# A delta rule with a dense layer behind it: the order of weight loads, of the second block's Y, of a merge step and of the lane copies

## The chip, the cores and the metric

One core of one Trainium2 chip runs the whole kernel. The metric is the device time of one execution in microseconds (us), the median of several runs. The engines are named as in the profile: PE is TensorE (matmuls), PEld its weight loads, ACT is ScalarE, DVE is VectorE, POOL is GpSimd, and SP is the engine that only issues transfers here. ACT and POOL have transfer queues of their own.

## What is computed

Every one of 4x8 heads runs a linear-attention recurrence with the delta rule over 768 steps, with a state of 48x48. Its output, put side by side over the heads, goes through a dense layer of 384 to 2048, a piecewise activation, and a second one back to 384.

```python
k_n = k / (np.linalg.norm(k, axis=-1, keepdims=True) + 1e-06)
for t in range(S):                       # S = 768, state starts at zero
    kt, vt, bt = (k_n[:, :, t], v[:, :, t], beta[:, :, t, None])
    y[:, :, t] = np.einsum('bhd,bhde->bhe', q[:, :, t], state)
    v_old = np.einsum('bhde,bhd->bhe', state, kt)
    state = state + bt[:, :, :, None] * np.einsum('bhd,bhe->bhde', kt, vt - v_old)
x = y.transpose(0, 2, 1, 3).reshape(3072, 384)
h = x @ w_in                             # 384 -> 2048
g = np.where(h >= 1, h, np.where(h <= -1, 0.0, (h + 1) ** 2 / 4))
out = g @ w_out                          # 2048 -> 384
```

All is float32; the dense products are done in three passes over a high and a low part.

## The kernel before

**Blocks and pairs.** Time is cut into 12 blocks of 64 steps, and two blocks make a pair: six pairs, G = 0 to 5. In a block the recurrence becomes a triangular solve and a few products. For every block: the Gram products of the keys (`gram_k`, into GG) and of queries with keys (`gram_q`, into Q); the inverse of a unit triangular 64x64 matrix; and the chain of four products through the state: R (`chain_r`, values less what the state holds), U (`chain_u`), Y (`chain_y`, the output, written as a high and a low part into xb), and D (`chain_d`, the state update). Y needs U; D needs U; the next block's R needs D; U needs R.

**The inverse.** `lanes` copies the 32x32 diagonal parts of GG beside themselves (L266), transposes them to lanes on DVE (L268), computes the norms (with a square root on ACT, L236), scales (L281) and lets POOL cut the triangle (L282). `solve` or `solve_whole` eliminates column by column on DVE (L300 to L313), `unlanes` brings the result back into XT and GG. Then `merge32` joins two 32x32 inverses to one of 64 on PE: its first argument names the block whose first product y1 (L374) is made, its second the block whose second product x2 (L376) is made. y1 is evicted to GG on ACT (L386), and x2 of the same block reads that. x2 is evicted to XT (L381), which U reads. `merge16_a` and `merge16_b` do the same a level below, in the first two pairs only.

**The dense layers.** For each pair there are 16 *items*, one per 128 of the 2048 hidden columns. An item is the up projection (L610, nine matmuls of 512 columns into h), the activation (two passes and a square on ACT, L735 and L754, and a maximum on DVE, L762), the split into ghi (ACT, L730) and glo (DVE, L731), and, two items later, the down projection (L625, twelve matmuls). h has two banks, so an up waits for the maximum of two items before. The first pair has 24 items: eight for its first block alone, eight for both, eight for its second block alone; those for one block are half as wide.

**The order around the items.** All engines take their work in program order. `at(pe, G, t, ...)` puts a product, and `at(fill, G, t, ...)` a piece of other work (a step of a generator, a load), at item t of pair G; t goes in halves. On PE, a product at a whole t stands between the up and the down of that item, one at t + 0.5 stands behind the down. The product at a whole t is evicted in the same item, ahead of the second activation pass; the one at t + 0.5 at the beginning of the next item (`finish(late)`). The fills of the same half stand ahead of the eviction on ACT and DVE. `M` is the item at which the merge steps of the pair begin, 16 in the first pair and 8.5 in the others. While pair G's items run, the recurrence of pair G + 1 is worked off. The solve for the pair after that starts at item -1.5, that is, in the last items of the pair before.

**The seam.** Y of a block goes to xb partly by copies and partly through a small tile, stg, which six transfers on SP's queue (L461) put in their rows: r = 0 and 64, and for each the three parts k. The first up of the next pair reads xb part by part; its first part needs the first and the fourth transfer.

**The prologue.** Before the items, the first two blocks are loaded: K by halves on SP and ACT, Q and KV on SP. The first three of sixteen weight tiles (768 KB each) go on ACT's queue ahead of Q in the program, the next five on SP behind Q. While DVE solves, PE runs 36 holding matmuls (`hold`, L554, 72 instructions) behind the Q-K products. `stage` runs products on PE, then some steps of weight unpacking (`wu`, on ACT and DVE) or of scaling (`sv`), then the evictions. The PSUM tiles `ch` have two banks, which all pieces of the chain take in turn.

Of the kernel before, what the change touches and what calls it, by code (L numbers as in the profile page):

```python
# [24 lines left out]
SOON = 8  # L25
# [6 lines left out]
def delta_rule_moe(ctx: ExitStack, tc: tile.TileContext, kqa, kqb, kv, beta, w, out):  # L32
# [14 lines left out]
    nc = tc.nc  # L47
# [58 lines left out]
    def weight_loads(n0, n1, q=nc.sync):  # L106
        for f in range(n0, n1):
            RAW[f] = const.tile([P, 2, 2 * DM], F32, name=f"wt{f}")
            q.dma_start(out=RAW[f].bitcast(I32), in_=w.bitcast(I32)[:, f])
# [1 line left out]

    load_k(0, (nc.sync, nc.scalar))
    load_k(1, (nc.sync, nc.scalar))
    weight_loads(0, 3, nc.scalar)
    beta_sb = const.tile([P, NS, 32], F32, name="beta_sb")
    nc.sync.dma_start(out=beta_sb[:, 0], in_=beta[:, 0])
    load_q(0)
    load_q(1)
    weight_loads(3, SOON)
    load_kv(0)  # L120
    load_kv(1)
    load_k(2)
# [3 lines left out]
    for c0, base, step, n in ((0, -H, -C, NP), (NP, -C - H - NP, C, NP), (C, -C, C, H)):  # L126
        x = perm[:, 0:C].rearrange("c (a f l) -> c a f l", f=2, l=H)[:, :, :, c0:c0 + NP] if c0 < C else perm[:, C:P].rearrange("c (a f l) -> c a f l", f=2, l=H)
# [29 lines left out]
    GG = const.tile([P, 2, NU, C], F32, name="GG")  # L157
# [30 lines left out]
    def banks(*shape):  # L188
        return [ps.tile([P, H, *shape], F32, **acc()) for _ in range(2)]
# [4 lines left out]
    def gram_k(g):  # L194

        x, b_ = KE.pop(g) if g in KE else K[g], banks(C)
        for j in range(H):
            for e, f in quarters():
                k, o = x[f * C:f * C + D, e * H + j, :], (1 - e) * C
                nc.tensor.matmul(b_[f][o:o + C, j], k, k, start=True, stop=True)  # L200

        def evict():
            for f in range(2):
                nc.scalar.copy(out=GG[:, g % 2, half(f)], in_=b_[f])
        return evict
# [48 lines left out]
    def lanes(G):  # L254

        A = S["A"] = sb.tile([P, 32, 32], F32, name="A", bufs=1)
        if G < WHOLE:
            X = S["X"] = sb.tile([P, 2, 16, 16], F32, name="X", bufs=1)
            Xf = X.rearrange("l s c t -> l (s c t)")
            nc.gpsimd.memset(X, 0.0)  # L260
            for s in range(2):
                nc.gpsimd.memset(Xf[:, 256 * s:256 * s + 256:17], 1.0)
            nc.gpsimd.memset(ZT[:, :, :, 16:32], 0.0)
        for g in range(2):
            for r in (0, C):
                nc.vector.tensor_copy(out=GG[r:r + 32, g, :, 32:64], in_=GG[r:r + 32, g, :, 0:32])  # L266
            yield
        nc.vector.transpose(out=A, in_=GG[:, :, :, 32:64].rearrange("p g u t -> p t (g u)"))  # L268
        yield
        n = sb.tile([P, 32], F32, name="N2")  # L270
        nc.vector.tensor_copy(out=n, in_=A.rearrange("l j t -> l (j t)")[:, 0:1024:33])
        r = norms(n)
        N = S["N"] = sb.tile([P, 32], F32, name="N3")
        nc.vector.transpose(out=N, in_=n)
        gm = S["gm"] = sb.tile([P, 32], F32, name="gm")
        nc.vector.reciprocal(out=r, in_=n)
        nc.vector.tensor_tensor(out=gm, in0=r, in1=beta_sb[:, G, :], op=ALU.mult)
        nc.vector.tensor_tensor(out=gm, in0=gm, in1=r, op=ALU.mult)
        yield
        if G >= WHOLE:  # L280
            nc.vector.scalar_tensor_tensor(out=A, in0=A, scalar=-1.0, in1=gm[:, :, None].broadcast_to([P, 32, 32]), op0=ALU.mult, op1=ALU.mult)  # L281
            nc.gpsimd.affine_select(out=A, in_=A, pattern=[[-1, 32], [1, 32]], base=0, channel_multiplier=0,  # L282
                                    compare_op=ALU.is_gt, fill=0.0)
            nc.gpsimd.memset(A.rearrange("l c t -> l (c t)")[:, 0:1024:33], 1.0)
            return
        A16 = S["A16"] = sb.tile([P, 2, 16, 16], F32, name="A16", bufs=1)
        for s in range(2):
            b = slice(16 * s, 16 * s + 16)
            nc.vector.tensor_tensor(out=A16[:, s], in0=A[:, b, b], in1=gm[:, b, None].broadcast_to([P, 16, 16]), op=ALU.mult)
        X32 = S["X32"] = sb.tile([P, 32, 32], F32, name="A", bufs=1)  # L290
        nc.gpsimd.memset(X32, 0.0)
        yield
# [243 lines left out]
    def stage(pieces, *fill):  # L536
        evicts = products(*pieces)
        for gen, m in fill:
            run(gen, m)
        finish(evicts)  # L540

    spare += START
    wu, sv, ln, raws = unpack(), [scale_v(0), scale_v(1)], lanes(0), []
# [19 lines left out]
    one_ = lambda f, *a: [lambda: f(*a)]  # L563
# [1 line left out]
    stage(one_(merge16_a, 1), (wu, 4))  # L565
    stage(one_(merge16_b, 0), (sv[0], 2), (wu, 2))
    stage(one_(merge16_b, 1), (wu, 4))
    stage(one_(merge32, 0, None, True), (wu, 3))
    stage(one_(merge32, 1, 0, True), (wu, 3))
    stage(one_(merge32, None, 1), (wu, 1), (sv[1], 2))  # L570
    weight_loads(SOON, SOON + 2, nc.scalar)
    stage(both(chain_u, 0), (wu, 2))
    stage(both(chain_y, 0), (wu, 4))
# [61 lines left out]
    pe, fill = {}, {}  # L635

    def at(where, G, t, *x):
        where.setdefault(2 * first[G] + int(round(2 * t)), []).extend(x)

    def lane_steps(G, t, gen, *more):  # L640
        for j in (0,) + (more or (0.5, 1, 1.5, 2)):
            at(fill, G, t + j, (gen, 1))

    def chain(G, t, a):
        for j, f, g in ((0, chain_u, a), (1, chain_y, a), (2, chain_d, a), (3, chain_r, a + 1), (4, chain_u, a + 1), (4.5, chain_y, a + 1), (5.5, chain_d, a + 1)):
            if (f, g) != (chain_d, ntot - 1):
                at(pe, G, t + j, lambda f=f, g=g: f(g))

    def plan(G):

        a, b = 2 * G + 2, 2 * G + 3
        if G == NS - 1:
            return
        va, vb = scale_v(a), scale_v(b)
        if G == 0:
            ln, so, un = lanes(1), solve(), unlanes()
            at(pe, G, 0, lambda: chain_y(1))
            at(fill, G, 0.5, (load_q, 3))
            at(pe, G, 0.5, lambda: chain_d(1))
            at(pe, G, 1, lambda: place_beta(1, NS))  # L660
            at(fill, G, 1, (load_kv, 3))
            at(pe, G, 1.5, lambda: gram_k(a))
            at(pe, G, 2.5, lambda: gram_k(b))
            lane_steps(G, 7, ln)
            for j in range(8):
                at(fill, G, 9.5 + j / 2, (so, 2))
            at(pe, G, 11.5, lambda: gram_q(a))
            at(pe, G, 12.5, lambda: gram_q(b))
            at(fill, G, 13.5, (un, 1))
            at(fill, G, 13.5, (un, 9))  # L670
            for j in range(2):
                at(fill, G, 10 + j, (va, 1))
                at(fill, G, 16 + j, (vb, 1))
            at(pe, G, 13.5, lambda: chain_r(a))
            M = 14
            for j, f in enumerate((merge16_a, merge16_b)):
                for g in range(2):
                    at(pe, G, M + j + g / 2, lambda f=f, g=g: f(g))
            M = 16
            last = 24  # L680
        else:
            so, un = solves.pop(G)
            at(fill, G, 0.5, (va, 1))
            at(fill, G, 1, (va, 1))
            at(pe, G, 2.5, lambda: chain_r(a))
            at(pe, G, 4.5, lambda: gram_q(a))
            at(pe, G, 6, lambda: gram_q(b))
            cost, hs = 0, 0
            for j in range(1, 31):
                at(fill, G, -1.5 + hs / 2, (so, 1))  # L690
                cost += j * (31 - j) + 150
                hs = int(cost / 9461 * 17)
            for j, t in enumerate((7, 7.5, 8, 8)):
                at(fill, G, t, (un, 1))
            at(fill, G, 9, (vb, 1))
            at(fill, G, 9.5, (vb, 1))
            M = 8.5
            last = 16
        for j, x in enumerate(((0, None), (1, 0), (None, 1))):
            at(pe, G, M + j / 2, lambda x=x: merge32(*x))  # L700
        chain(G, M + 1.5, a)
        if G < NS - 2:
            at(fill, G, 6.5 if G else 14, (load_k, a + 2))
            at(fill, G, M + 0.5, (load_k, b + 2, (nc.sync, nc.sync), True))
            at(pe, G, M + 2, lambda: gram_k(a + 2))
            at(pe, G, M + 4, lambda: gram_k(b + 2))
            lane_steps(G, M + 3, lanes(G + 2), 1.5, 2, 2.5, 3)
            solves[G + 1] = solve_whole(), unlanes_whole()
            at(fill, G, M + 3.5, (load_q, a + 2))
            at(fill, G, M + 5, (load_k, b + 2))  # L710
            at(fill, G, M + 7, (load_q, b + 2))
            at(fill, G, last + 0.5, (load_kv, a + 2))
            at(fill, G, last + 1.5, (load_kv, b + 2))

    solves = {}
    for G in range(NS):
        plan(G)
# [20 lines left out]
    for n, item in enumerate(items):  # L738
# [16 lines left out]
        if len(ready) == LAG:  # L755
            x = ready.pop(0)
# [11 lines left out]
    G = NS - 1  # L768
# [50 lines left out]
```

## Time and profile before

| | us |
|---|---|
| runs before, median of 3 | 662.41 |
| runs before, lowest and highest | 660.76, 667.59 |
| profiled execution | 666.11 |
| its span from first to last instruction | 664.4 |
| mean granted TensorE clock | 0.928 |

The profile is of one execution. A busy time is the sum over an engine's instructions, an idle time in brackets is what stood just before the instruction on its engine, with what seems to have released it. A line number is that of the kernel before. The items of the six pairs begin at about 82, 211, 305, 399, 495 and 585 us; in each, PE is busy for nearly all of the time, and the places where it is not are what the prediction quotes.

### The profile page before, as it was taken

The numbers are of one execution on the slowest core, as the hardware profiler recorded it, in microseconds if no ns is written. First come the engines' busy times: TensorE is split into PE (matmuls) and PEld (weight loads), VectorE is DVE, ScalarE is ACT, GpSimd is POOL, SyncE is SP. The second block draws the span as 40 slices with busy tenths as digits, with TensorE's granted clock in tenths as the row PEclk, the third lists the DMA queues.
The fourth block names the chain that finished last, engine by engine and source line by source line (L and its number), as shares of the span: only waits on it lengthen the run. The fifth ranks groups of instructions, "written<-read, shape, count | busy, mean of one in ns | idle before, by whom it ended". The sixth has DMA issues, their size and how long they took to land.

```text
span 664.4 us, 21796 instructions
## 1 busy us (share of the span) xinstructions
PE 605.8 (91%) x9584; PEld 523.5 (79%) x9584; DVE 423.0 (64%) x882; ACT 379.7 (57%) x659; POOL 30.2 (5%) x62
## 2 busy tenths in 40 slices
PE   6985787898897999998999989999979999989996
PEld 5745675687786888887888878888868888879995
DVE  3587969994258894467992577872677854333332
ACT  2315667653754658664569554568545577556663
POOL 2003000000002000010000020000020000000000
PEclk8595679997998999998999998999989999989998
DMA  8720494001022411013400114310214100001001
GB/s 245 280 82 10 165 299 111 8 6 51 9 64 68 113 28 29 17 52 86 110 21 22 42 34 108 93 28 3 66 34 112 38 2 10 6 23 39 0 1 47
DMA packets 32430, 42.54 MB, mean 64 GB/s; under 512 B 7056, under 2 KB 27152, under 8 KB 32336
## 3 DMA queue, kind: packets, MB, share of 16 engines
q1 hardware_dynamic: 30768, 36.64, 19.8%
q10 hardware_dynamic: 1312, 4.42, 2.0%
q8 instruction: 75, 1.23, 0.7%
q14 instruction: 19, 0.16, 0.1%
q0 software_dynamic: 256, 0.08, 0.1%
HBM read 34.05 MB, written 4.72 MB: 58 GB/s over the span
## 4 chain that ended last, share of the span: by engine, by line
PE 67%; DVE 11%; ACT 10%; issue 4%; DMA 4%; SPq 2%; POOL 1%; DVEq 0%; POOLq 0%; ACTq 0%
PE h L610 25%; PE o L625 25%; PE ch L554 4%; PE ch L431 3%; ACT GG L386 2%; ACT XT L381 2%; DMA Q<-in_kqb_dram 2%; ACT XT L388 2%; SPq L461 2%; PE ch L213 2%; PE ch L396 1%; DVE s L762 1%; PE ch L412 1%; ACT s L735 1%; PE ch L200 1%
## 5 line engine op out<-in xcount | busy, mean ns | idle before, releaser
L610 PE MATMUL h<-xb,wt 128*128 128x512 f32 (+1 forms) x936 | 232.8, 395 | 21.1 <-DMA xb<-X 8.4
L610 PEld LDWEIGHTS h<-xb,wt 128*128 128x128 f32 x936 | 170.2, 196 | 55.5 <-issue 9.8
L625 PE MATMUL o<-wt,ghi 128*128 128x384 f32 x768 | 204.1, 348 | 0.0
L625 PEld LDWEIGHTS o<-wt,ghi 128*128 128x128 f32 x768 | 140.7, 193 | 7.4
L762 DVE TENSOR_TENSOR s<-h,s 128x512 f32<-128x512 f32 (+1 forms) x104 | 67.1, 645 | 105.8 <-ACT s L754 105.1
L625 PE MATMUL o<-wt,glo 128*128 128x384 f32 x384 | 131.8, 343 | 0.5 <-DVE glo L731 0.5
L735 ACT ACTIVATE s<-h,half 128x512 f32<-128x512 f32 (+1 forms) x104 | 68.2, 655 | 86.0 <-PE h L610 85.7
L730 ACT CAST ghi<-s 128x512 fp32r<-128x512 f32 (+1 forms) x104 | 61.4, 590 | 83.7 <-DVE s L762 76.4
L731 DVE TENSOR_TENSOR glo<-s,ghi 128x512 fp32r<-128x512 f32 (+1 forms) x104 | 67.0, 644 | 54.5 <-ACT ghi L730 54.4
L625 PEld LDWEIGHTS o<-wt,glo 128*128 128x128 f32 x384 | 74.0, 193 | 2.2 <-DVE glo L731 2.2
L735 ACT ACTIVATE s<-s,one 128x512 f32<-128x512 f32 (+1 forms) x104 | 72.1, 693 | 2.6
L754 ACT ACTIVATE s<-s 128x512 f32<-128x512 f32 (+1 forms) x104 | 62.3, 599 | 3.3
L311 DVE TENSOR_TENSOR pr<-A 128x30 f32<-128x30 f32 (+14 forms) x120 | 39.4, 328 | 6.3 <-POOL A L282 4.5
L313 DVE TENSOR_TENSOR A<-A,pr 128x30 f32<-128x30 f32 (+14 forms) x120 | 39.9, 332 | 4.4
L431 PEld LDWEIGHTS ch<-Q,SU 64*64 64x64 f32 (+3 forms) x1056 | 24.0, 142 | 5.0 <-issue 1.3
L431 PE MATMUL ch<-Q,SU 64*64 64x64 f32 (+3 forms) x1056 | 26.3, 230 | 1.1 <-ACT SU L416 1.1
L457 DVE TENSOR_TENSOR xb<-ch,xb 128x384 fp32r<-128x384 f32 x22 | 12.2, 552 | 19.3 <-ACT X L452 14.4
L554 PE MATMUL ch<-SU 128*128 128x64 f32 (+1 forms) x72 | 24.4, 528 | 0.0
L376 PE MATMUL ch<-GG 32*32 32x32 f32 x768 | 18.2, 200 | 5.0 <-ACT GG L386 5.0
L554 PEld LDWEIGHTS ch<-SU 128*128 128x128 f32 x72 | 15.3, 281 | 8.4 <-issue 8.3
L376 PEld LDWEIGHTS ch<-GG 32*32 32x32 f32 x768 | 15.9, 113 | 7.3 <-ACT GG L386 7.3
L451 ACT CAST xb<-ch 128x384 fp32r<-128x384 f32 x22 | 10.7, 489 | 17.9 <-PE ch L431 17.9
(128 smaller groups left out, 600.7 us busy)
## 6 DMA issues: line engine op xcount, KB each, us to landing
wt<-in_w_dram SPq DMA_DIRECT2D x11, 768.0 KB, 7.0
out_dram<-wx SPq DMA_DIRECT2D x47, 96.0 KB, 2.2
wt<-in_w_dram ACTq DMA_DIRECT2D x5, 768.0 KB, 6.9
KV<-in_kv_dram SPq DMA_DIRECT2D x36, 96.0 KB, 2.4
KV<-in_kv_dram SPq DMA_DIRECT2D x72, 48.0 KB, 2.3
KV<-in_kv_dram SPq DMA_DIRECT2D x12, 192.0 KB, 2.7
xb<-X SPq DMA_DIRECT2D x66, 32.0 KB, 2.0
K<-in_kqb_dram SPq DMA_DIRECT2D x12, 128.0 KB, 3.1
```

Source lines behind the costliest of these rows:

```text
L311: nc.vector.tensor_tensor(out=pr, in0=A[:, 0:n, j:j + 1].broadcast_to([P, n, m]), in1=A[:, j:j + 1, j + 1:32].broadcast_to([P, n, m]), op= ...
L313: nc.vector.tensor_tensor(out=A[:, 0:n, j + 1:32], in0=A[:, 0:n, j + 1:32], in1=pr, op=ALU.add)
L376: nc.tensor.matmul(x2[r:r + 32, u], GG[r:r + 32, gb, u, 32:64], GG[r:r + 32, gb, u, 0:32], start=True, stop=True)
L431: nc.tensor.matmul(yy[i][o * C:o * C + C, e, p], SF[rows, u:u + C], w_[rows, x, k, :], **how)
L554: nc.tensor.matmul(idle[:, 0:m], SF[:, 0:P], SF[:, 0:m], start=True, stop=True)
L610: nc.tensor.matmul(h[:, cols(bs)], WT[f][:, 0, x, k * P:(k + 1) * P], XB[G][:, y, k, cols(bs)], start=(n == 0), stop=(n == 8))
L625: nc.tensor.matmul(oacc[G, k], (ghi, glo)[x][:, k * P:(k + 1) * P], WT[f][:, 1, y, :], start=(new and n == 0), stop=(left[G, b] == 0 and n ...
L730: nc.scalar.copy(out=ghi[:, c], in_=s[:, c])
L731: nc.vector.tensor_tensor(out=glo[:, c], in0=s[:, c], in1=ghi[:, c], op=ALU.subtract)
L735: nc.scalar.activation(out=out, in_=in_, func=AF.Relu, bias=bias, scale=scale)
L754: nc.scalar.activation(out=s[:, c], in_=s[:, c], func=AF.Square)
L762: nc.vector.tensor_tensor(out=s[:, c], in0=h[:, c], in1=s[:, c], op=ALU.max)
```

## The change

Nothing that is computed changes. The edits:

- The weight tiles 0 to 2 leave ACT's queue; tiles 0 to 7 are all loaded on SP, behind Q.
- `lanes` makes its four copies per pair on ACT rather than DVE, except in the prologue.
- In the prologue, three merge stages become four: the first products of both blocks, then the second ones, with the same number of weight steps over all.
- In the items, `merge32(None, 1)` moves from M + 1 to M + 2.5. The chain, still beginning at M + 1.5, has all that follows its first U half an item earlier: the second block's Y comes at item 14 in the later pairs, where it was 14.5.
- The Gram products of the keys for the pair after next come an item and half an item earlier, the first lane step an item, and two loads of Q half an item.
- In pair 1 the solve begins at -0.5 rather than -1.5, its steps spread over 15 half items rather than 17.

```diff
     load_k(1, (nc.sync, nc.scalar))
-    weight_loads(0, 3, nc.scalar)
     beta_sb = const.tile([P, NS, 32], F32, name="beta_sb")
...
     load_q(1)
-    weight_loads(3, SOON)
+    weight_loads(0, SOON)
...
-                nc.vector.tensor_copy(out=GG[r:r + 32, g, :, 32:64], in_=GG[r:r + 32, g, :, 0:32])
+                (nc.scalar.copy if G else nc.vector.tensor_copy)(out=GG[r:r + 32, g, :, 32:64], in_=GG[r:r + 32, g, :, 0:32])
...
-    stage(one_(merge32, 0, None, True), (wu, 3))
-    stage(one_(merge32, 1, 0, True), (wu, 3))
-    stage(one_(merge32, None, 1), (wu, 1), (sv[1], 2))
+    stage(one_(merge32, 0, None, True), (wu, 2))
+    stage(one_(merge32, 1, None, True), (wu, 2))
+    stage(one_(merge32, None, 0), (wu, 3))
+    stage(one_(merge32, None, 1), (sv[1], 2))
...
-        for j, f, g in ((0, chain_u, a), (1, chain_y, a), (2, chain_d, a), (3, chain_r, a + 1), (4, chain_u, a + 1), (4.5, chain_y, a + 1), (5.5, chain_d, a + 1)):
+        for j, f, g in ((0, chain_u, a), (0.5, chain_y, a), (1.5, chain_d, a), (2.5, chain_r, a + 1), (3.5, chain_u, a + 1), (4, chain_y, a + 1), (5, chain_d, a + 1)):
...
-                at(fill, G, -1.5 + hs / 2, (so, 1))
+                at(fill, G, (-0.5 if G == 1 else -1.5) + hs / 2, (so, 1))
                 cost += j * (31 - j) + 150
-                hs = int(cost / 9461 * 17)
+                hs = int(cost / 9461 * (15 if G == 1 else 17))
...
-        for j, x in enumerate(((0, None), (1, 0), (None, 1))):
-            at(pe, G, M + j / 2, lambda x=x: merge32(*x))
+        for j, x in ((0, (0, None)), (0.5, (1, 0)), (2.5, (None, 1))):
+            at(pe, G, M + j, lambda x=x: merge32(*x))
...
-            at(pe, G, M + 2, lambda: gram_k(a + 2))
-            at(pe, G, M + 4, lambda: gram_k(b + 2))
-            lane_steps(G, M + 3, lanes(G + 2), 1.5, 2, 2.5, 3)
+            at(pe, G, M + 1, lambda: gram_k(a + 2))
+            at(pe, G, M + 3.5, lambda: gram_k(b + 2))
+            lane_steps(G, M + 2, lanes(G + 2), 2.5, 3, 3.5, 4)
...
-            at(fill, G, M + 3.5, (load_q, a + 2))
+            at(fill, G, M + 3, (load_q, a + 2))
             at(fill, G, M + 5, (load_k, b + 2))
-            at(fill, G, M + 7, (load_q, b + 2))
+            at(fill, G, M + 6.5, (load_q, b + 2))
```

## The prediction

> **What bounds the kernel now.** I read the page first, then the windows, the timeline at the seams between the pairs of blocks, and the chain of waits.
>
> ```profile
> PE 605.8 (91%) x9584; PEld 523.5 (79%) x9584; DVE 423.0 (64%) x882; ACT 379.7 (57%) x659; POOL 30.2 (5%) x62
> ```
>
> TensorE is busy for 605.8 of 664.4 us, so some 59 us of idle time, and the time at a lower clock, are what a new order can win. The windows (columns: stretch, its length, then busy time of PE, PEld, DVE, ACT, POOL, granted clock, DMA share, GB/s) say where:
>
> ```profile
> 20.00:45.00 25.00, 25.00 (x115) 15.83 (x111) 21.07 (x55) 3.43 (x6) 0.96 (x1) 0.74 0.67 228
> 110.00:120.00 10.00, 6.30 (x35) 4.80 (x35) 9.93 (x16) 6.61 (x14) 0.00 (x0) 1.00 0.34 89
> 170.00:180.00 10.00, 8.82 (x238) 7.81 (x241) 1.79 (x4) 9.18 (x17) 0.00 (x0) 1.00 0.01 3
> 304.00:399.00 95.00, 90.91 (x1424) 78.98 (x1424) 65.60 (x145) 57.07 (x97) 3.51 (x6) 0.98 0.20 54
> ```
>
> A later pair (304 to 399) has 4.1 us of idle PE in 95. Nearly all of it lies at the seam to the next pair. Here is the seam from the second pair to the third, by engine:
>
> ```profile
> 293.57 2.24 PE L431 MATMUL ch<-Q,SU 112*64 112x64 f32 x96
> 295.75 2.34 PE L610 MATMUL h<-xb,wt 128*128 128x512 f32 x9
> 300.10 1.57 PE L473 MATMUL ch<-SU,KV 64*48 64x48 f32 x64
> 304.72 3.20 PE L610 MATMUL h<-xb,wt 128*128 128x512 f32 x9 [3.05 <-DMA xb<-X]
> ...
> 295.85 0.48 ACT L451 CAST xb<-ch 128x384 fp32r<-128x384 f32 x1 [1.71 <-PE ch L431]
> ...
> 294.78 1.22 DVE L281 SCALAR_TENSOR_TENSOR A<-A,gm 128x1024 f32<-128x1024 f32 x1
> 297.51 0.19 DVE L311 TENSOR_TENSOR pr<-A 128x30 f32<-128x30 f32 x1 [1.50 <-POOL A L282]
> 298.98 0.55 DVE L457 TENSOR_TENSOR xb<-ch,xb 128x384 fp32r<-128x384 f32 x1
> ...
> 300.46 3.88 SPq L461 DMA_DIRECT2D xb<-X  x6
> ```
>
> Y's products end at 295.81 and ScalarE starts on them at once, but VectorE's half (L457) waits in its queue behind L281, the wait for GpSimd's select, and three solve steps, until 298.98. So the six transfers start at 300.46, 4.65 us after Y. The next pair's first up projection needs the fourth of them. The other seams and the chain of waits:
>
> ```profile
> 211.11 3.32 PE L610 MATMUL h<-xb,wt 128*128 128x512 f32 x7 [2.54 <-DVE SU L488]
> ...
> 399.15 4.18 PE L610 MATMUL h<-xb,wt 128*128 128x512 f32 x9 [3.00 <-issue]
> ...
> 495.11 4.18 PE L610 MATMUL h<-xb,wt 128*128 128x512 f32 x9 [3.46 <-DMA xb<-X]
> ...
> 585.16 3.66 PE L610 MATMUL h<-xb,wt 128*128 128x512 f32 x9 [1.86 <-DMA xb<-X]
> ```
>
> ```profile
> 302.47 2.01 DMA xb<-X
> ...
> 307.93 2.76 PE o L625 x12
> 310.69 2.10 PE h L610 x9
> 312.79 2.08 PE o L625 x12
> ...
> 403.33 2.85 PE o L625 x12
> ...
> 499.29 2.66 PE o L625 x12
> ...
> 588.82 2.30 PE o L625 x12
> ```
>
> The wait is paid twice: after it the first up takes 3.20 to 4.18 us where 2.10 is usual, and the first down 2.30 to 2.85 where 2.08 is. Those are matmuls at a halved clock (4.18 is twice 2.09). The extra is 1.10+0.68, 2.08+0.77, 2.08+0.58 and 1.56+0.22 us at the last four seams: 1.78, 2.85, 2.66 and 1.78.
>
> **The prologue.**
>
> ```profile
> 6.01 1.62 ACTq L109 DMA_DIRECT2D wt<-in_w_dram  x3
> ...
> 4.26 0.47 SPq L87 DMA_DIRECT2D Q<-in_kqb_dram  x1
> ...
> 14.58 0.66 SPq L92 DMA_DIRECT2D Q<-in_kqa_dram  x1
> 17.70 2.58 SPq L109 DMA_DIRECT2D wt<-in_w_dram  x5
> 20.32 1.45 SPq L98 DMA_DIRECT2D KV<-in_kv_dram  x1
> ...
> 33.37 0.60 SPq L98 DMA_DIRECT2D KV<-in_kv_dram  x1
> ...
> 37.20 0.58 SPq L101 DMA_DIRECT2D KV<-in_kv_dram  x1
> ...
> 20.38 24.45 PE L554 MATMUL ch<-SU 128*128 128x64 f32 x72
> ...
> 22.25 0.18 DVE L237 TENSOR_SCALAR r<-y 128x32 f32<-128x32 f32 x1 [8.12 <-ACT y L236]
> 44.73 1.02 DVE L248 TENSOR_TENSOR KV<-KV,N 128x384 f32<-128x384 f32 x2
> ```
>
> ```profile
> q10 hardware_dynamic: 232, 1.31, 89.6%
> q1 hardware_dynamic: 157, 0.14, 11.6%
> ```
>
> The last fence is the DMA view from 10 to 14 us. Three weight tiles on ACT's queue (q10) hold the engines, SP's queue (q1) with Q gets a ninth, and Q's last issue comes only at 14.58. VectorE idles 8.12 us and the holding matmuls (L554) begin only at 20.38. The weight unpacking that fills VectorE later (9.93 of 10 us between 110 and 120) is placed by program order behind the same work, so what the prologue wins passes through it.
>
> **The change, part by part.** *Weights on SP behind Q.* Q's twelve issues run from 4.26 on. Alone on the engines they should be spaced as the seven of KV from 33.37 to 37.20: 0.64 us. The last is then issued at about 11.3, not 14.58. If the 5.80 us from there to the holds (14.58 to 20.38) stay, the holds start at 17.1, 3.3 us earlier; if Q lands as fast as xb later (2.01) and half of its products, an estimated 1.2, are left, at 14.6, 5.8 earlier. Nothing at all is won if the holds, at a mean clock of 0.74 between 20 and 45, stay at the halved clock so much longer: bounds 0 and 5.8. I take 5.0, nearer the upper end, for those 5.80 us contain the crowding that goes (11.6% of the engines for q1). Eight weights then stand ahead of KV on SP: at the most 3 x 0.52 (2.58 over 5) = 1.5 us of issue. KV is first used at 44.73, without a wait, now near 39.7; its first transfers were issued at 20.32. That cover is large, so nothing.
> [...]
>
> *Four merge stages for three in the prologue.*
>
> ```profile
> 63.61 0.31 PE L376 MATMUL ch<-GG 32*32 32x32 f32 x2 [1.85 <-ACT GG L386]
> ```
>
> The second block's first product no longer carries the first block's second, so ScalarE frees GG sooner and this 1.85 us wait shrinks. But the weight steps (same 30 in all) and an XT copy now stand before U: a gain between -1 and 1.85; I take 1.0.
>
> *Y of the second block at item 14.* It moves ahead of a down projection: 2.08 us earlier on PE. Its evictions come before L281, the select and the solve. Between Y's end and the transfers stand two of ScalarE's four casts (the first 0.48 us), what is left of the norms on VectorE, and VectorE's own four operations (298.98 to 300.46, 1.5 us): an estimated 3.4, where 4.65 were. The fourth transfer is issued 2.0 later and lands after 2.01: Y's end + 7.4, and PE sees it at 7.6. PE's own work in between is now down, up, state update, down: 2.08+2.10+1.57+2.08 = 7.8. The wait is gone with 0.2 to spare, and with it the halved clock. What is late next is VectorE around the seam (state update, three to four solve steps, the max that frees h): I charge 0.5 us a seam, bounds 0 and 1.5. So: second to third 3.05+1.78-0.5 = 4.3; 399: 3.00+2.85-0.5 = 5.35; 495: 3.46+2.66-0.5 = 5.6; 585, where no solve stands by: 1.86+1.78 = 3.6. Sum 18.9.
> The first seam (211) follows half-wide items. There Y moves past half a down, 1.04 us, and the norms stay ahead of it on VectorE: I take 1.5 (bounds 0 and 2.54), with the halved clock left in.
> [...]
>
> *Chain half an item earlier, merge step behind the first Y, Gram steps and loads earlier.* PE does the same instructions. U and Y of the first block now stand apart by one down (2.08 us), as the second block's do, and each other piece by an up or down that covers its eviction. In the half-wide items of the first pair one cover is 1.05, so U to Y and Y to the merge lose a little: I take -1.0, bounds -3 and 1. SP meets each load behind Y's transfers as before: nothing.
>
> *Lane copies.*
>
> ```profile
> L266 DVE COPY GG<-GG 32x512 f32<-32x512 f32 x24 | 9.9, 413 | 7.2 <-ACT GG L204 6.9
> L388 ACT COPY XT<-XT 32x512 f32<-32x512 f32 x20 | 12.3, 616 | 0.4
> ```
>
> Twenty copies leave VectorE (8.3 us) for ScalarE (20 x 0.616 = 12.3). ScalarE has 38 us free in a pair of 95, so nothing on the path beyond the norms' delay counted above.
> *Third pair's solve an item later.* Thirty steps over 15 half items for 17, same end: nothing.
>
> Sum: 5.0+1.0+18.9+1.5-1.0 = 25.4 us. The profiled execution took 666.11 (span 664.4 and 1.7 around it) and would take 640.7. It stands 0.56% above the median of 662.41, from which the sum gives 637.0, my forecast.
>
> **The rivals.** *Y's transfers still come last* (chance 0.18). The margin of 0.2 rests on VectorE's norms, which wait for ScalarE, now with copies in its queue. If the transfers are 2 us later at the three seams with a solve, 1.9 us of wait and the halved clock (2.43 on average) stay: 3 x 4.3 = 13 less, 650. For it: L457 sat 1.9 us behind other work already. Against: L281 and the select go behind it.
> *The prologue gains nothing* (0.10): the holds run longer by what they start earlier. 662.4-19.4 = 643. For it: the clock of 0.74; against: it is the same 72 matmuls.
> *ScalarE becomes the bound, and the kernel is slower* (0.06). Copies and Y's eviction stand ahead of the second activation of the same item, whose square releases the max that frees h. If all is on the path, 12.3 + 5 x 1.2 = 18 us are added, the seams win nothing, the prologue's 6 stay: 674. It decides where ScalarE is above nine tenths busy. For it: 9.18 of 10 us between 170 and 180; against: 57 of 95 in later pairs.
>
> **How the numbers follow.** The forecast, 637 (own range 630 to 645), has 0.60; the rivals 0.18, 0.10 and 0.06; 0.06 is for mixtures about no change. The lower end takes the first seam's clock (2.9, as at 399), the seam charge (1.5) and two to three us of the prologue and first pair: 629. The upper end is the first rival with 2 us: 652. About 1%, 6.6 us, is what a measurement of this kernel can tell from no change: faster 0.87, within it 0.08, slower 0.05.
>
> **What would show it.** Right: hold matmuls from about 15; VectorE's wait for L236 near 2 us; no PE wait above 0.5 us and clock 1.0 at the last four seams; up after the seam at 2.1; Y's transfers issued some 3.4 us after Y. Wrong: a wait for xb that stays, a new one for L762 or on ch at items 9 to 12, holds that end at 45, ScalarE full in the first pair's tail.

## The result and the profile after

| | time, median (lowest to highest) | profiled execution | its span | granted clock |
|---|---|---|---|---|
| before | 662.01 us (660.76 to 667.59) | 666.11 us | 664.4 us | 0.928 |
| changed | 640.32 us (639.83 to 641.19) | 640.05 us | 638.3 us | 0.954 |

The ratio is 0.9658, with a 95% interval of 0.9602 to 0.9714: 21.7 us less on the medians, 26.1 us between the two profiled executions. Of the changed kernel's page, first the busy times, then the TensorE clock in 40 slices (tenths), and below it the clock of the kernel before:

```profile
PE 596.0 (93%) x9584; PEld 514.9 (81%) x9584; DVE 413.8 (65%) x862; ACT 389.9 (61%) x679; POOL 29.7 (5%) x62
...
PEclk8685579999999999999999999999999999999999
...
PEclk8595679997998999998999998999989999989998
```

PE's busy time fell by 9.8 us although it does the same 9584 matmuls: that goes with the lower clock, whose dips past the first slices are gone. Its idle time fell by 16 us. The windows (columns as before) say in which stretches:

```profile
20.00:45.00 25.00, 23.16 (x422) 14.09 (x422) 20.12 (x45) 3.88 (x7) 0.30 (x1) 0.84 0.67 227
110.00:120.00 10.00, 8.14 (x37) 6.09 (x35) 7.53 (x11) 8.12 (x16) 0.00 (x0) 1.00 0.03 8
170.00:180.00 10.00, 9.63 (x257) 8.73 (x256) 4.05 (x10) 8.81 (x22) 0.00 (x0) 1.00 0.18 43
304.00:399.00 95.00, 93.45 (x1502) 80.61 (x1502) 66.97 (x148) 61.54 (x105) 3.51 (x6) 1.00 0.23 60
```

The 95 us of the later pairs hold 93.45 us of PE for 90.91, at a clock of 1.00 for 0.98. The seam from the second pair to the third, by engine:

```profile
282.47 2.24 PE L430 MATMUL ch<-Q,SU 112*64 112x64 f32 x96
...
284.64 0.62 PE L625 MATMUL o<-wt,ghi 128*128 128x384 f32 x2
284.75 0.48 ACT L450 CAST xb<-ch 128x384 fp32r<-128x384 f32 x1 [0.80 <-PE ch L430]
...
286.07 0.55 DVE L456 TENSOR_TENSOR xb<-ch,xb 128x384 fp32r<-128x384 f32 x1
...
286.83 2.24 PE L610 MATMUL h<-xb,wt 128*128 128x512 f32 x9
...
287.55 3.87 SPq L460 DMA_DIRECT2D xb<-X  x6
288.00 1.21 DVE L280 SCALAR_TENSOR_TENSOR A<-A,gm 128x1024 f32<-128x1024 f32 x1
...
289.00 1.15 PE L472 MATMUL ch<-SU,KV 64*48 64x48 f32 x64
...
290.72 0.19 DVE L310 TENSOR_TENSOR pr<-A 128x30 f32<-128x30 f32 x1 [1.51 <-POOL A L281]
...
292.27 2.26 PE L610 MATMUL h<-xb,wt 128*128 128x512 f32 x9
```

(Line numbers up to some L609 are one lower than before.) VectorE's half of Y's eviction, L456, now stands ahead of L280 and the wait for GpSimd, so the six transfers start at 287.55, 2.8 us after Y's end (4.65 before), and the up at 292.27 waits for nothing: the fourth transfer, which it needs, lands at 291.77, half a microsecond ahead. The next three seams and the first one:

```profile
201.86 2.34 PE L610 MATMUL h<-xb,wt 128*128 128x512 f32 x9 [1.26 <-DVE A L312]
...
383.06 2.26 PE L610 MATMUL h<-xb,wt 128*128 128x512 f32 x9
...
474.53 2.33 PE L610 MATMUL h<-xb,wt 128*128 128x512 f32 x9 [0.49 <-DVE glo L731]
...
560.69 2.29 PE L610 MATMUL h<-xb,wt 128*128 128x512 f32 x9
```

No up of 3 to 4 us is left, and three seams are free of a wait for xb. At the other two a short one remains. The profile puts these waits of 1.26 and 0.49 us down to VectorE, but what came last was a transfer, as the same kernel run again shows:

```profile
202.52 2.35 PE L610 MATMUL h<-xb,wt 128*128 128x512 f32 x9 [1.06 <-DVE pr L310]
...
474.82 2.34 PE L610 MATMUL h<-xb,wt 128*128 128x512 f32 x9 [0.53 <-DVE glo L731]
```

There the fourth transfer, issued at 200.35 and 471.41, lands at 202.32 and 474.73, 0.2 and 0.1 us ahead of these ups; in the kernel before, at the first seam, it lands at 210.91, 0.2 ahead of the up at 211.11. At 471.41 it takes 3.3 us to land rather than 2.0. Why is open. The clock stays up at both (1.00 from 200 to 206 and from 473 to 479 us in the changed kernel). The prologue:

```profile
11.32 0.42 SPq L92 DMA_DIRECT2D Q<-in_kqa_dram  x1
11.78 5.01 SPq L109 DMA_DIRECT2D wt<-in_w_dram  x8
14.46 9.75 PE L553 MATMUL ch<-SU 128*128 128x64 f32 x41
16.33 0.18 DVE L236 TENSOR_SCALAR r<-y 128x32 f32<-128x32 f32 x1 [3.43 <-ACT y L235]
38.81 1.02 DVE L247 TENSOR_TENSOR KV<-KV,N 128x384 f32<-128x384 f32 x2
```

Q's last issue is at 11.32 for 14.58, the holding matmuls begin at 14.46 for 20.38, and KV, behind eight weights on SP, is still used without a wait.

What is new on the path stands some two items behind a seam, first at 208 to 214, behind the first seam, then at 303, behind the second:

```profile
208.32 0.56 DVE L247 TENSOR_TENSOR KV<-KV,N 128x384 f32<-128x384 f32 x1 [1.25 <-DMA KV<-in_kv_dram]
...
213.59 0.55 DVE L631 COPY wx<-o 128x384 f32<-128x384 f32 x1
...
214.19 0.62 PE L625 MATMUL o<-wt,ghi 128*128 128x384 f32 x2 [1.77 <-DVE wx L631]
...
303.33 0.62 PE L625 MATMUL o<-wt,ghi 128*128 128x384 f32 x2 [0.42 <-ACT wx L631]
...
303.93 1.01 DVE L631 COPY wx<-o 128x384 f32<-128x384 f32 x2
304.54 0.61 PE L625 MATMUL o<-wt,ghi 128*128 128x384 f32 x2 [0.42 <-DVE wx L631]
```

The down that opens the next pair's accumulators waits for the copies (L631) that store the pair before. VectorE reaches them late, behind solve steps, and at 208 behind KV's landing too. The start of every up, before minus after, gives where the 26.1 us came from:

| stretch (items) | forecast | gain |
|---|---|---|
| to the first up (81.65 to 75.41) | 5.0 + 1.0 | 6.2 |
| first pair (0 to 23) | -1.0 | 0.5 |
| first seam (23 to 26) | 1.5 | 5.2 |
| behind it: KV and store (26 to 28) | 0 | -2.4 |
| second to third pair (28 to 43) | 4.3 | 3.1 |
| third to fourth (43 to 59) | 5.35 | 4.7 |
| fourth to fifth (59 to 75) | 5.6 | 5.0 |
| fifth to last (75 to 91) | 3.6 | 3.7 |
| sum | 25.4 | 26.1 |

### The profile page after: what moved, and what is told of

It is laid out like the page before. It is cut to its first block, busy times and chain, and to the rows that moved or that the text cites. A ratio compares the mean times of both kernels' runs of the same rounds, so it can differ in the third digit from the quotient of the medians.

```text
span 638.3 us, 21794 instructions
## 1 busy us (share of the span) xinstructions
PE 596.0 (93%) x9584; PEld 514.9 (81%) x9584; DVE 413.8 (65%) x862; ACT 389.9 (61%) x679; POOL 29.7 (5%) x62
## 3 DMA queue, kind: packets, MB, share of 16 engines
q10 hardware_dynamic: 880, 2.07, 1.0%
## 4 chain that ended last, share of the span: by engine, by line
PE 57%; DVE 21%; ACT 10%; issue 6%; DMA 3%; SPq 2%; POOL 1%; DVEq 0%; ACTq 0%
PE o L625 20%; PE h L610 18%; PE ch L553 4%; PE ch L430 3%; DVE glo L731 3%; DVE pr L310 3%; DVE A L312 2%; DVE s L762 2%; ACT s L735 2%; ACT GG L385 2%; PE ch L395 2%; ACT XT L387 2%; PE ch L375 2%; DVE SU L487 1%; DVE A L267 1%
## 5 line engine op out<-in xcount | busy, mean ns | idle before, releaser
L610 PE MATMUL h<-xb,wt 128*128 128x512 f32 (+1 forms) x936 | 226.1, 387 | 8.5 <-DVE s L762 5.8
L625 PE MATMUL o<-wt,ghi 128*128 128x384 f32 x768 | 200.9, 343 | 3.9 <-DVE wx L631 3.0
L610 PEld LDWEIGHTS h<-xb,wt 128*128 128x128 f32 x936 | 165.4, 191 | 41.6 <-DVE s L762 7.8
L625 PEld LDWEIGHTS o<-wt,ghi 128*128 128x128 f32 x768 | 137.2, 189 | 12.9 <-DVE wx L631 4.3
L625 PE MATMUL o<-wt,glo 128*128 128x384 f32 x384 | 130.3, 339 | 0.6 <-DVE glo L731 0.5
L625 PEld LDWEIGHTS o<-wt,glo 128*128 128x128 f32 x384 | 72.4, 189 | 2.3 <-DVE glo L731 2.3
L456 DVE TENSOR_TENSOR xb<-ch,xb 128x384 fp32r<-128x384 f32 x22 | 12.1, 551 | 14.5 <-ACT X L451 10.2
L226 DVE TENSOR_TENSOR Q<-ch,mask 64x512 f32<-64x512 f32 (+1 forms) x30 | 20.6, 687 | 0.4
L281 POOL TENSOR_SCALAR_AFFINE_SELECT A<-A 128x1024 f32<-128x1024 f32 x4 | 5.1, 1264 | 299.5 <-DMA xb<-X 261.1
L487 DVE TENSOR_TENSOR SU<-ch,SU 48x384 f32<-48x384 f32 (+1 forms) x30 | 16.6, 555 | 0.7 <-PE ch L472 0.3
```

Source lines behind the costliest of these rows:

```text
L487: nc.vector.tensor_tensor(out=x, in0=y, in1=x, op=ALU.add)
L610: nc.tensor.matmul(h[:, cols(bs)], WT[f][:, 0, x, k * P:(k + 1) * P], XB[G][:, y, k, cols(bs)], start=(n == 0), stop=(n == 8))
L625: nc.tensor.matmul(oacc[G, k], (ghi, glo)[x][:, k * P:(k + 1) * P], WT[f][:, 1, y, :], start=(new and n == 0), stop=(left[G, b] == 0 and n ...
```

## The experiments

Each stands beside runs of the kernel before on its own chip; each "changed kernel" below is the one that this document is about.

**Weights back on ScalarE's queue.** The prologue alone is undone, in the changed kernel:

```diff
+    weight_loads(0, 3, nc.scalar)
     beta_sb = ...
-    weight_loads(0, SOON)
+    weight_loads(3, SOON)
```

> The changed kernel (640.3 us) with weight tiles 0 to 2 back on ACT's queue ahead of Q. Theory: Q lands late again, the holding matmuls begin near 20 us instead of 14.5, and all that follows moves with them: about 646 (645 to 647.5), with the first up near 81.5. Rival: the time up to the first up is set by VectorE's weight unpacking or by PE's own issue, so that an earlier Q is only waited for later: 640 to 642.

648.32 us (645.45 to 649.52), ratio 0.9762 (0.9712 to 0.9811). Its timeline:

```profile
20.49 3.89 PE L554 MATMUL ch<-SU 128*128 128x64 f32 x17
...
22.36 0.18 DVE L237 TENSOR_SCALAR r<-y 128x32 f32<-128x32 f32 x1 [8.17 <-ACT y L236]
```

The 8.17 us wait and the late holds are back, the first up comes at 81.72, 6.3 us later, and the end is 8.0 us later on the median. The time is 0.8 us above the band, and the first up is where it was expected. Where three transfers are issued is, in these profiled executions, the whole of the prologue's gain. In the profiled execution the end is 9.5 us later; the three beyond the 6.3 lie behind the first seam; what takes them is not shown.

**Y half an item later.** The changed kernel, with the second block's U, Y and D back at their old times:

```diff
-... (3.5, chain_u, a + 1), (4, chain_y, a + 1), (5, chain_d, a + 1)
+... (4, chain_u, a + 1), (4.5, chain_y, a + 1), (5.5, chain_d, a + 1)
```

> The changed kernel with U, Y and D of the second block half an item later again (14, 14.5 and 15.5), all else as changed. Theory: at four seams VectorE's half of Y stands behind L281, the select and three solve steps again, PE waits some 3 us for xb and the clock halves: 13 to 17 us more, 653 to 658, the clock lower at each of the last four seams. Rival: the gain at the seams came from the other moves (lane copies on ScalarE, the merge step), Y alone gives only its 2 us at a few seams: 642 to 646.

662.84 us (656.99 to 666.26), ratio 0.9979 (0.9941 to 1.0017): 22.5 us for half an item, and nothing left of the gain although the prologue keeps its six. The direction was expected, not the size. The second seam of this kernel, on PE, VectorE and SP's queue:

```profile
286.79 2.28 PE L430 MATMUL ch<-Q,SU 112*64 112x64 f32 x96 [0.23 <-ACT SU L415]
289.16 1.22 DVE L280 SCALAR_TENSOR_TENSOR A<-A,gm 128x1024 f32<-128x1024 f32 x1
...
291.88 0.19 DVE L310 TENSOR_TENSOR pr<-A 128x30 f32<-128x30 f32 x1 [1.50 <-POOL A L281]
...
293.36 0.55 DVE L456 TENSOR_TENSOR xb<-ch,xb 128x384 fp32r<-128x384 f32 x1
...
294.83 2.60 SPq L460 DMA_DIRECT2D xb<-X  x4
```

```profile
299.09 2.47 PE L610 MATMUL h<-xb,wt 128*128 128x512 f32 x5 [3.04 <-DMA xb<-X]
```

L456 is behind L280, the select and three solve steps again, the transfers start 5.8 us after Y's end, and the wait of 3.04 us is there. Against the changed kernel this one loses 2.0 us up to behind the first seam, then 5.5, 5.0, 6.9 and 3.6 at the four later seams: 21.0, where the prediction had 18.9 for them and the change won 16.5 (table above). So with the other moves in place the old time of Y is 4.5 us worse there than the kernel before, which takes most of the prologue's six as well: L456 ends up 4.3 us behind Y's end, where L457 stood 3.2 behind it before, and at three seams the state update (L472) waits for the eviction too, 0.8 to 1.0 us and again 0.4. That Y half an item earlier (with its U and D) is what removes these waits, lower clock and all (five products of the up at 299.09 take 2.47 us, where the changed kernel's nine at 292.27 take 2.26), is shown.

**Only the chain's times, in the kernel before.**

```diff
-... (1, chain_y, a), (2, chain_d, a), (3, chain_r, a + 1), (4, chain_u, a + 1), (4.5, chain_y, a + 1), ...
+... (0.5, chain_y, a), (1.5, chain_d, a), (2.5, chain_r, a + 1), (3.5, chain_u, a + 1), (4, chain_y, a + 1), ...
```

> The kernel before with the chain's new times alone (first Y, D, R, U, Y, D half an item earlier); weights, merges, lanes, Gram steps, loads and solve as before. Theory: this part carries the seams, 13 to 17 us: 645 to 649, and no PE wait above 1 us at the last four seams. Rival: it needs the moved merge step and the copies on ScalarE, for without them ch or VectorE makes PE wait at items 10 to 13 instead: 653 to 660.

663.01 us (659.99 to 666.12), ratio 0.9984 (0.9956 to 1.0013): nothing. The theory fell. The rival is right that PE waits on ch instead, but its band ended 3 us lower, and its copies on ScalarE turn out not to be needed (next run). Its timeline in the second pair's items, and a row of its waits (total, times, longest):

```profile
268.35 2.24 PE L431 MATMUL ch<-Q,SU 112*64 112x64 f32 x96
...
271.98 0.55 DVE L457 TENSOR_TENSOR xb<-ch,xb 128x384 fp32r<-128x384 f32 x1
272.16 0.30 PE L200 MATMUL ch<-K 48*64 48x64 f32 x2 [1.57 <-issue]
272.82 1.50 PE L200 MATMUL ch<-K 48*64 48x64 f32 x62 [0.37 <-issue]
274.25 2.07 PE L610 MATMUL h<-xb,wt 128*128 128x512 f32 x4
```

```profile
PE ch L200 <- issue: 7.7, 8, 1.6
```

The waits at the four later seams are gone here too. But Y of the first block and the Gram product gram_k (L200) now fall into the same half item, and gram_k has to wait until Y's result has been read out of the same ch banks. The profile names no releaser, but VectorE's two readings of Y end (L458) at 272.06 and 272.72, each 0.1 us ahead of a start of gram_k. Behind the two at 272 the clock falls (0.88 from 268 to 282 us, where the changed kernel has 1.00 from 260 to 274), four products of the up at 274.25 take 2.07 us, and what the seams win is lost in mid-pair.

**All of the new order, in the kernel before.** As the last one, and with the merge step, Gram products, lane steps and loads at their new places; prologue, lane copies and the third pair's solve stay old:

```diff
+        for j, x in ((0, (0, None)), (0.5, (1, 0)), (2.5, (None, 1))):
+            at(pe, G, M + j, lambda x=x: merge32(*x))
...
+            at(pe, G, M + 1, lambda: gram_k(a + 2))
+            at(pe, G, M + 3.5, lambda: gram_k(b + 2))
```

> The kernel before with all of the new order of the pairs (chain half an item earlier, the third merge step behind the first Y, the Gram products, lane steps and loads at their new places), but with its old prologue, its lane copies on VectorE and the old solve of the third pair. Theory: the order is one thing; with the Gram and merge moves beside the chain's times the pairs win what they won in the changed kernel, and only the prologue's 6.2 us are missing: no wait of PE above 0.6 us for Gram's banks (L200), clock 1.0 at the last four seams, first up near 81.7, time 645.5 to 649. Rival, that the lane copies on ScalarE or the later solve are needed for it: ScalarE's or VectorE's lateness brings a wait at the seams or at the lane steps back, 650 to 658.

644.84 us (643.87 to 646.64), ratio 0.9703 (0.9654 to 0.9753), below the band by less than a microsecond. The same 95 us of its windows, and the prologue on PE:

```profile
304.00:399.00 95.00, 93.74 (x1444) 80.71 (x1444) 68.74 (x153) 60.04 (x103) 3.51 (x6) 1.00 0.22 58
```

```profile
13.90 1.68 PE L213 MATMUL o<-Q,K 48*64 48x64 f32 x32 [3.79 <-DMA Q<-in_kqb_dram]
```

The order wins the seams by itself: 93.74 us of PE, clock 1.00; in the old prologue PE still waits 3.79 us for Q. The moves that the prediction priced at nothing or less (Gram, the merge step, lane steps and loads) are worth 18 us together with the chain's times, and those times without them are worth nothing. Which of these moves is needed was not run apart; the waits of the last run point at Gram. The first up comes at 82.03, 6.6 us behind the changed kernel; 4.4 of it are left at the end, most of the difference because here no 1.77 us wait for a store stands at 214.

**Lane copies back on VectorE,** in the changed kernel:

```diff
-                (nc.scalar.copy if G else nc.vector.tensor_copy)(out=GG...
+                nc.vector.tensor_copy(out=GG...
```

> The changed kernel with the lane copies back on VectorE in all pairs. Theory: at the copies' items both engines have gaps, and the norms may even start 1 us earlier; VectorE is not full before the seam: 639.5 to 641.5. Rival: VectorE's 1.65 us more per pair arrive at the seam, where the state update and the solve already delay the maximum and the stores: 642 to 646, with longer PE waits at items 0 to 2 of each pair.

640.19 us (638.70 to 641.91), ratio 0.9646 (0.9600 to 0.9693): no difference, as the prediction had it.

**Three merge stages in the prologue,** in the changed kernel:

```diff
-    stage(one_(merge32, 0, None, True), (wu, 2))
-    stage(one_(merge32, 1, None, True), (wu, 2))
-    stage(one_(merge32, None, 0), (wu, 3))
-    stage(one_(merge32, None, 1), (sv[1], 2))
+    stage(one_(merge32, 0, None, True), (wu, 3))
+    stage(one_(merge32, 1, 0, True), (wu, 3))
+    stage(one_(merge32, None, 1), (wu, 1), (sv[1], 2))
```

> The changed kernel with the three old merge stages of the prologue in place of four. Rival, the prediction's term: the first up comes 1.0 us later (76.4) and the time is 641.3. Theory after the traces: the fourth stage's gain is there at the first U (some 1.2 us) and is lost again in the gaps of 0.9 and 1.4 us without a releaser ahead of Y and U, so the first up starts within 0.4 us of 75.4 and the time is 640 to 640.8.

641.75 us (641.27 to 643.52), ratio 0.9660 (0.9617 to 0.9704). Its timeline, and then the changed kernel's:

```profile
57.17 0.31 PE L375 MATMUL ch<-GG 32*32 32x32 f32 x2 [1.85 <-ACT GG L385]
...
72.22 2.07 PE L411 MATMUL h<-KV,XT 64*64 64x48 f32 x64 [2.44 <-issue]
75.21 2.29 PE L609 MATMUL h<-xb,wt 128*128 128x256 f32 x9 [0.92 <-ACT SU L415]
```

```profile
72.41 2.07 PE L411 MATMUL h<-KV,XT 64*64 64x48 f32 x64 [1.44 <-issue]
75.41 2.29 PE L610 MATMUL h<-xb,wt 128*128 128x256 f32 x9 [0.92 <-ACT SU L415]
```

The 1.85 us wait for GG is back, and yet the first up is not later, as the theory had it. The time, 640 to 640.8 by that theory, is 1.2 to 1.4 us above the changed kernel's two medians, near the 641.3 of the prediction's term, but they were not run beside this one on its chip, and against the kernel before on its own chip the ratio of 0.9660 is within 0.001 of the changed kernel's 0.9658 and 0.9653. The profile can't decide it either, since the first up comes anywhere from 74.4 to 76.5 in the profiled executions that share the changed weight loads, and this execution also lost the clock at 147 (0.84 us for two products of a down at 147.91, where 0.51 is usual). What the fourth stage is worth, nothing or a microsecond, is open.

**The new wait: all store copies on ScalarE,** for the first four pairs of the changed kernel, alone and together with an earlier load:

```diff
-            (nc.scalar.copy, nc.vector.tensor_copy)[k % 2](out=o[:, k % 2], in_=oacc[G, k])
+            (nc.scalar.copy if G < NS - 1 else (nc.scalar.copy, nc.vector.tensor_copy)[k % 2])(out=o[:, k % 2], ...
...
-            at(fill, G, last + 0.5, (load_kv, a + 2))
+            at(fill, G, last + 0.5 if G else 21.5, (load_kv, a + 2))
```

> The changed kernel with all four store copies of the first four pairs (L631) on ScalarE in place of two on ScalarE and two on VectorE. Theory: at the seams a down waits for the store's copy on VectorE, which stands behind the norms and the solve there (0.42 us twice a seam in the trace, some 1.4 us with what surrounds it); ScalarE has room, so the wait for L631 falls below 0.3 us a seam and the time by 2 to 4 us, to 636.5 to 638.5. Rival: ScalarE's casts and evictions then stand behind four copies (4 x 0.47 us), the wait only changes its engine, and the time is 640 to 642.

> The last one with the first pair's load of KV (a+2) issued at item 21.5 rather than 24.5 as well. Theory: VectorE's 1.25 us wait for KV at 208 and the 1.77 us wait of PE at 214 behind it go, so that the gain of 12 us over the kernel before that items 25 and 26 show is kept past item 27 (9.55 there in the changed kernel): 1 to 2.4 us below the run with the store copies alone. Rival: the earlier load meets the transfers of Y at the first seam on the queue or the store's copy is late for another reason; no difference above 0.5 us.

The copies alone: 640.03 us (638.38 to 642.13), ratio 0.9627 (0.9586 to 0.9669). Both: 637.76 us (637.38 to 639.77), ratio 0.9599 (0.9559 to 0.9639). A group of the first one's page (busy, mean, idle before it):

```profile
L625 PE MATMUL o<-wt,ghi 128*128 128x384 f32 x768 | 201.3, 344 | 0.8 <-ACT wx L631 0.8
```

The wait for L631 fell from 3.9 to 0.8 us, and each of three seams won 0.6 to 0.7 us, half of the 1.4 that the theory had. The time did not follow: in the profiled execution the clock fell at 170 and at 249 (the Gram products at 170.07 took 1.97 us, 1.15 in the changed kernel; the up at 248.24 took 3.89), in the first and the second pair, and the two stretches lost 2.6 us each, more than the seams won; whether this edit or chance brings that is open. The band up to 638.5 was missed by the copies alone. With the early load the time is 2.3 us lower on the same chip, as that theory had it, though the two ranges overlap.

**The load alone, and the copies on ScalarE in the later pairs only,** with the changed kernel once more on the same chip:

```diff
-            (nc.scalar.copy, nc.vector.tensor_copy)[k % 2](...
+            (nc.scalar.copy if 0 < G < NS - 1 else (nc.scalar.copy, nc.vector.tensor_copy)[k % 2])(...
```

> The changed kernel once more, beside the next three on the same chip, so that differences of some 2 us can be read against it. Both theories: 639.5 to 641.5. [...]

> The changed kernel with the load of KV (a+2) of the first pair at item 21.5 rather than 24.5, and nothing else. Theory: VectorE's waits for KV at 208 and 212 (1.25 and 0.74 us) go, with them PE's 1.77 us wait for the store's copy at 214, and the time is 1 to 2.4 us below the changed kernel's, 638 to 639.5. Rival: the gain at 638 of the run with both edits comes from the stores alone, and this one equals the changed kernel.

> The early load of KV, and the store copies on ScalarE for the second, third and fourth pair only; the first pair's stay as they were. Theory: the three seams win 0.65 us each as in the runs before, KV's wait wins up to 2.4, and ScalarE's late squares of the half-wide items (VectorE waits 3.6 us for L754 near 205 in the run with all of them) are avoided: 1.5 to 4 us below the changed kernel's, 636 to 638.5. Rival: the same as the run with all pairs' copies on ScalarE, 637.5 to 638.5.

| kernel | time | ratio (95% interval) |
|---|---|---|
| changed, again | 640.54 us (639.00 to 641.75) | 0.9653 (0.9624 to 0.9683) |
| KV earlier | 639.90 us (637.74 to 641.96) | 0.9643 (0.9612 to 0.9673) |
| KV earlier, later pairs' copies on ScalarE | 637.03 us (636.45 to 641.39) | 0.9611 (0.9580 to 0.9642) |

The early load by itself misses its band by 0.4 us and can't be told from the changed kernel in time, though the 1.77 us wait at 214 is gone from its trace: its profiled execution lost as much to a lower clock at 170 (the Gram products at 169.84 took 1.86 us, 1.15 in the changed kernel). With the later pairs' copies five of six runs are below all six of the changed kernel, by 3.5 us on the medians; the two intervals overlap, so that it is faster is likely rather than settled, and it can't be told from the run with all copies on ScalarE and the early load (637.76 us on another chip, ratio 0.9599). Against the changed kernel's first profile the ups gain 2.2 us up to item 27 and 0.6, 0.7 and 0.7 where the store's copies stood behind three seams.

**Third pair's solve begun earlier,** as in the kernel before:

```diff
-                at(fill, G, (-0.5 if G == 1 else -1.5) + hs / 2, (so, 1))
+                at(fill, G, -1.5 + hs / 2, (so, 1))
...
-                hs = int(cost / 9461 * (15 if G == 1 else 17))
+                hs = int(cost / 9461 * 17)
```

> The changed kernel with the third pair's solve begun an item earlier, over 17 half items as in the kernel before. The prediction's term: nothing, within 0.5 us of the changed kernel's. Rival: its steps then stand ahead of Y's evictions and of the store's copies on VectorE in the first seam's items, as they do at the other seams, and 0.5 to 2 us are lost near 200 to 215.

639.09 us (638.34 to 640.84), ratio 0.9634 (0.9605 to 0.9664). The rival's sign is wrong: the store's wait near 215 is 0.32 us here, not longer, perhaps since with the later start more of the long steps stand ahead of that copy. 1.4 us on the medians, with overlapping runs: at the edge of what can be told, and if anything a small loss by the later solve. The prediction's term of nothing, within 0.5 us, is not met by the medians.

## Why the prediction was right, and where it was not

The forecast was 637.0 with a range of 629 to 652; the time is 640.32. The profiled execution was to fall to 640.7 and fell to 640.05. Step by step:

- **Weights on SP** (5.0): right. Holds were put at 14.6 at best and 17.1 at worst and began at 14.46, Q's last issue at 11.3 and came at 11.32. The term was a microsecond short, since the upper bound of 5.8 was what the trace then gave, 5.9. VectorE's wait for L236 is 3.43, not near 2, and the holds began on time all the same. The one queue's extra issues hid behind KV's slack, and from 20 to 45 us the transfers moved 227 GB/s where they had moved 228: order was what changed.
- **Four merge stages** (1.0): neither shown nor refuted. The medians differ by that much, the ratios and the profiles do not. Left open.
- **Y at item 14** (18.9 at four seams): the mechanism at the seam is what the trace shows: L456 ahead of L280, transfers 2.8 us behind Y (3.4 forecast), the fourth one landing 0.5 us ahead of the up (0.2 forecast), no lower clock (1.00 from 304 to 399 us). 16.5 were won, and putting Y back loses 21.0. The wait was not gone at one seam, 4 to 5, where 0.49 of it stays. The charge of 0.5 a seam for what is late next, VectorE around the seam, was mis-sized, and it was not the state update or the max but in the main the store's copies, two waits of 0.42 at 303; moving them to ScalarE won back 0.6 to 0.7:

| seam | wait and clock, forecast | measured | next wait, forecast | measured |
|---|---|---|---|---|
| 2 to 3 | 4.83 | 4.5 | 0.5 | 1.4 |
| 3 to 4 | 5.85 | 6.1 | 0.5 | 1.4 |
| 4 to 5 | 6.12 | 5.6 | 0.5 | 0.7 |
| 5 to 6 | 3.64 | 3.7 | 0 | 0 |

 (Measured: the item starts from 28, 43, 59 and 75 to 42, 58, 74 and 91, then to 43, 59 and 75.) The bound of 1.5 held it. Before, PE never waits for L631: the seam's wait for xb gave VectorE the time. Now PE comes sooner, and VectorE's queue is as long as it was.
- **First seam** (1.5, halved clock left in): mis-sized. The wait, for the fourth transfer before and after, shrank as said, from 2.54 to 1.26, but the clock stayed up (1.00 from 200 to 206 us), and 5.2 us were won. The wait of 1.86 us at 585 in the kernel before, behind which the clock is 0.50 from 585.8 to 589.1, was no measure for one of 1.26. With waits of 2.16 and 2.21 us at the first seam (Y half an item later; all copies on ScalarE with the early load) the clock fell: four products of the up took 2.05 us in the one and nine took 3.75 in the other, where the changed kernel's nine took 2.34. Behind the seam 2.4 were given back to KV's landing and the store, which the prediction had as hidden ("SP meets each load behind Y's transfers as before: nothing"): it checked the queue, not the time that VectorE would now be early by.
- **Chain, merge and Gram moves** (-1.0): in sum within the bounds, 0.5. But the price list hid what they are: the moves of Gram and of the merge step (with the lane steps and loads), priced as nothing, decide whether the 18 us are had at all. In the kernel before with the chain's times alone they are not. That each piece then has an up or a down to cover its eviction needs Gram to move out of Y's slot; the prediction did not name this condition.
- **Lane copies, third pair's solve** (0): right for the copies; the solve is at most 1.5 us the other way, at the edge of what can be told.
- **From the profiled execution to the median**: this is where the 3.3 us between 637.0 and 640.32 lie. The sum was 25.4 against 26.1 measured on the profiled executions. So close a hit is partly luck: 3.7 too little at the first seam and 1.5 too little in the first pair stand against 2.4 too much behind the first seam and 2.4 too much at the later ones. On the medians only 21.7 were won, and the prediction subtracted its sum whole. The profiled execution of before stood 4.1 us above its median. The terms that were larger in it than in a middling run can't be told from one profile; the likeliest are the two windows of lower clock at 152 and 210 (0.50 from 152.3 to 159.1 and from 210.3 to 217.1), as the granted clock of the kernel before differs from one execution to the next: 0.940 in one of 660.54 us, 0.926 in one of 667.44.

Of the rivals, none came as a whole. Y's transfers still come last at the first seam and at 4 to 5, but with 1.26 and 0.49 us and the clock up; the prologue won; ScalarE is at 61%.

## What to carry to other kernels

A half item in a hand-written order can be worth the whole change (22.5 us here), when it decides on which side of long work in an engine's order (here L280, the select and solve steps on VectorE, 289.16 to 293.36 us with Y half an item later) an eviction stands; read what is queued ahead of the last producer before anything else. Price a move also by what it makes room for: pieces that share banks and fall into the same slot can take back what the earlier piece has won, as gram_k's waits of 1.57 and 0.37 us behind Y did. When a sum is made against one profiled execution, look where that one stands among the runs, and don't carry terms over whole which hang on the clock.

## What was not expected of the hardware

The same wait can cost differently. PE's wait for KV in the first pair, in the changed kernel run again and in the run with early KV and later stores:

```profile
147.33 1.26 PE L344 MATMUL ch<-XT,GG 32*32 32x16 f32 x128 [2.20 <-DVE KV L401]
148.52 0.62 PE L625 MATMUL o<-wt,ghi 128*128 128x384 f32 x2
```

```profile
145.40 1.26 PE L344 MATMUL ch<-XT,GG 32*32 32x16 f32 x128 [2.16 <-DVE KV L401]
146.59 1.01 PE L625 MATMUL o<-wt,ghi 128*128 128x384 f32 x2
```

The same 2.2 us leave the clock alone in the first, and a lower one follows them in the second (the first two products of the down take 1.01 us for 0.62). Ten profiled executions have the changed weight loads and this wait, of 2.13 to 2.20 us. In six of them the later pairs of such products in this down take 0.51 us each; in four, pairs of 0.84 us follow. So the length of the wait does not decide alone here. A lower clock also stands behind shorter ones: behind the 1.86 us at 585 in the kernel before (0.50 from 585.8 to 589.1), and behind the 1.57 and 0.37 us at 272 in the kernel with the chain's times alone (0.88 from 268 to 282). What else decides is not shown.

The kernels with such waits at the seams also scatter more: 656.99 to 666.26 us over ten runs with Y half an item later, 639.00 to 641.75 over six without the waits.
